# Two-dimensional FFT mixing and a gated FFN on one core: where the column transforms wait, when the last third of the down weights is loaded, and in which blocks the column sums run

## The chip, the core and the metric

The kernel runs on one core of one Trainium2 chip. A core has a matrix engine (TensorE, PE in the profile, with its weight loads listed as PEld), a vector engine (VectorE, DVE), an activation engine (ScalarE, ACT), a general engine (GpSimd, POOL) and a sync engine (SyncE, SP), which in this kernel issues nearly all DMAs. Each engine works through its own list of instructions in order, and the lists meet at semaphores. Matrix products land in PSUM; everything else lies in SBUF, 128 partitions wide. The metric is the device time of one launch in microseconds (us).

## What is computed

The input `x` has 2048 tokens of 576 channels, in bf16. The FFN widens to 4608.

```python
def _A_ref(x, w_r, w_i):                    # a learned filter in the frequency domain
    X = rfft2(x.astype(float32), axes=(-2, -1))
    X = X * (w_r + 1j * w_i)
    return irfft2(X, s=(S, D), axes=(-2, -1)).astype(bfloat16)

def _B_ref(x, w_gate, w_up, w_down):        # gated FFN
    return (_gelu(x @ w_gate) * (x @ w_up)) @ w_down

h  = x + _A_ref(_layernorm(x), A_w_r, A_w_i)
h2 = h + _B_ref(_layernorm(h), B_w_gate, B_w_up, B_w_down)
return h2
```

## The kernel before

**Tiling.** Token `p*16 + h` lies on partition `p`, row `h`, so the residual `h_sb` is 128 partitions x 16 rows x 576 channels. The FFT half (until about 79 us in the profile) does the forward transform, the product with the filter and most of the inverse transform as matrix products with tables of sines. Its last step is a pair: `inv_cols(x, g)` makes the inverse column transform for one of two halves `x` and one of eight pairs of rows `g` in PSUM and evicts it, and `add_rows(g)` with `add_h` (L668 to L694) adds the rows `2g` and `2g+1` of the result to `h_sb`. For `g` = 0 and 1 the evicted values are used at once. For `g` = 2 to 7 they are parked in fp32 as `cw[x, g]` (L576 to L584), and the FFN starts while they are parked. For `x` = 0, and for `g` = 2, each has a tile of its own. The five with `x` = 1 and `g` = 3 to 7 lie in one tile, `cwb` (L640), which shares its place with `wd_c`, the last third of the down weights: `wd_c` can be loaded only when `cwb` has been read for the last time.

`fold(g)` (L656) turns the parked values into bf16 sums and differences, the tile `both`, by four vector instructions (L664 and L665, once for each `x`). These are the column sums. `add_both(g)` issues the eight small matrix products `y_ps` (L678) on `both`, and then two vector adds into `h_sb` (L689). `stats2(h)` takes mean and variance of a finished row on VectorE and the reciprocal root on GpSimd; `norm2(h)` (L703) normalises the row into `hrow`; `flip(h)` (L715) transposes it by DMA into `hl`, the FFN's input, on SP. Rows 0 and 1 are flipped before the FFN, rows 2 and 3 are transposed on TensorE by `turn` at the same time.

**The FFN** runs over four chunks of four rows. A chunk has 36 blocks, one per 128 hidden columns. A block is 18 matrix products `gu` (L814), for gate and up, then GELU on ScalarE (L822) into `g_sb`, then the product with the up half on VectorE (L823) into `P_sb`, which has 36 columns of blocks. After the 36 blocks come 288 products `acc` with the down weights (L834), 12 blocks of hidden columns from each of `wd_a`, `wd_b` and `wd_c`, then the residual add (L846) and the store.

**Buffers and queues.** PSUM has four tiles of one kind ("two", L435), which `gu`, `y_ps` and `acc` take in turn, so the order of their allocation decides who waits for whom. Gate and up weights come in groups of three blocks (`load_gu`, L143, two DMAs of 432 KB each) into three buffers in turn: group `n` can be issued when the last product on group `n-3` is done. All these DMAs, the flips and the down weights stand in one list on SP, in program order: what waits at its head holds up the rest.

**The order around the change.** `todo` (L785) is a plan by block number, counted over all chunks. A block's entries are issued right behind its VectorE product. In the first chunk it places:

- `fold(2)` to `fold(7)` in blocks 2, 3, 4, 5, 6 and 7;
- `add_both(2)` to `add_both(7)` in blocks 4, 10, 16, 22, 28 and 34, and `stats2` of their two rows in the blocks after each;
- `norm2` and `flip` of rows 4 to 7 in blocks 14/15, 17/18, 20/21 and 23/24 (those of later rows in later chunks);
- `last_wd` in block 12, which loads `wd_c`.

Of the kernel before, what the change touches and what calls it, by code (L numbers as in the profile page):

```python
# [10 lines left out]
ALU = mybir.AluOpType  # L11
FP32 = mybir.dt.float32
BF16 = mybir.dt.bfloat16
# [7 lines left out]
P = 128  # L21
S = 2048
H = 16
D = 576
DH = D // 2
J = D // 2 + 1
JP = J + 1
JH = JP // 2
F = 4608
NFT = F // P  # L30
# [10 lines left out]
def kernel_body(  # L41
# [12 lines left out]
    V = nc.vector  # L54
# [11 lines left out]
    def two(name):  # L66
        return psum.tile([P, 2, 512], FP32, name=name, tag="two", bufs=3)
# [75 lines left out]
    def load_gu(g):  # L143
        gc = slice(g % (NFT // FQ) * FQ * P, (g % (NFT // FQ) + 1) * FQ * P)
        t = wgpool.tile([P, NR, FQ * P], BF16, name="wgu", tag="wgu")
        for c, w in ((0, B_w_gate), (1, B_w_up)):
            nc.sync.dma_start(t[64 * c : 64 * c + 64, :, :], w[:, gc].rearrange("(r k) c -> k r c", k=64))
        return t
# [12 lines left out]
    NWA = 12  # L161
    wd_a = keep.tile([P, NWA, D], BF16, name="wd_a")
# [400 lines left out]
    def inv_cols(x, g):  # L563

        ps = two("cs_ps")
        for e in range(2):
            for jt in range(NJT):
                T.matmul(  # L568
                    ps[:, e, 0:JP],
                    lhsT=EO[x][:, e, jt, 2 * g : 2 * g + 2].rearrange("p h e k l -> p (h e k l)"),  # L570
                    rhs=DT[:, jt, :, e, :] if jt < 2 else DI[:, :, e, :],
                    start=(jt == 0),
                    stop=(jt == NJT - 1),
                )
        pv = ps[:, :, 0:JP].rearrange("p t (q a) -> p t q a", q=2)
        if g >= 2:  # L576
            if x == 0 or g == 2:
                cw[x, g] = eop.tile([P, 2, JP], FP32, name=f"cw{x}{g}")[:]
            else:
                cw[x, g] = cwb[:, g - 3]  # L580
            A.activation(
                cw[x, g].rearrange("p t (a q) -> p t q a", q=2), pv, ACT.Copy, scale=Y_SCALE
            )
            return  # L584
        ts = [eop.tile([P, JP], BF16, name=f"cs{x}{g}{t}") for t in range(2)]
        for t in range(2):
            dst = ts[t][:].rearrange("p (a q) -> p q a", q=2)
            if x == 1 and t == 1:
                V.tensor_scalar(dst, pv[:, t], Y_SCALE, None, op0=ALU.mult)
            else:  # L590
                A.activation(dst, pv[:, t], ACT.Copy, scale=Y_SCALE)
        cs[x, g] = ts
# [43 lines left out]
    spw.__exit__(None, None, None)  # L636
    spec.__exit__(None, None, None)
    fp = ctx.enter_context(tc.tile_pool(name="ffn", bufs=1))
    P_sb = fp.tile([P, NFT, 4 * P], BF16, name="P_sb")
    cwb = fp.tile([P, 5, 2, JP], FP32, name="cwb", tag="wd2")[:]  # L640
    wd = [wd_a, fp.tile([P, NWA, D], BF16, name="wd_b")]

    def load_wd(i):
        nc.sync.dma_start(wd[i][:], wd_view[:, i * NWA : (i + 1) * NWA, :])

    def last_wd(h):
        wd.append(fp.tile([P, NWA, D], BF16, name="wd_c", tag="wd2"))
        load_wd(2)

    load_wd(1)  # L650

# [129 lines left out]
    turn(3)  # L781
    inv_cols(1, 6)
    inv_cols(1, 7)

    todo = {}  # L785
    for h in range(4, H):
        b = 6 * (h // 2 - 2)
        if h % 2 == 0:
            todo.setdefault(h // 2, []).append((fold, h // 2))
            todo.setdefault(b + 4, []).append((add_both, h // 2))  # L790
        todo.setdefault(b + 5 + h % 2, []).append((stats2, h))
        b = h // 4 * NFT - NFT + 3 * (h % 4) + 2 + 12 * (h < 8)
        todo.setdefault(b, []).append((norm2, h))
        todo.setdefault(b + 1, []).append((flip, h))

    todo.setdefault(12, []).append((last_wd, 0))

    blk = 0
    groups = pre
    NG = NFT // FQ  # L800
    for tcnk in range(4):
        for gi in range(NG):
            fa = gi * FQ
            w = groups.pop(0)
            n = tcnk * NG + gi + 2
            if 3 <= n < 4 * NG:
                groups.append(load_gu(n))
            for i in range(FQ):

                gu = two("gu")  # L810
                for r in range(NR):
                    for c in range(2):
                        rows = slice(64 * c, 64 * c + 64)
                        T.matmul(  # L814
                            gu[:, c, :],
                            lhsT=w[rows, r, i * P : (i + 1) * P],
                            rhs=hl[tcnk % 2][rows, r, :],
                            start=(r == 0),
                            stop=(r == NR - 1),
                        )  # L820
                g_sb = roll.tile([P, 4 * P], FP32, name="g_sb", tag="g_sb", bufs=3)
                A.activation(g_sb[:], gu[:, 0, :], ACT.Gelu_apprx_tanh)  # L822
                V.tensor_tensor(P_sb[:, fa + i, :], g_sb[:], gu[:, 1, :], ALU.mult)  # L823
                for fn, h in todo.pop(blk, ()):
                    fn(h)
                blk += 1
        for st in range(4):
            h = tcnk * 4 + st
            last = h == H - 1
            acc = two("acc")  # L830
            for c in range(2):
                cc = slice(c * DH, (c + 1) * DH)
                for f in range(NFT):
                    T.matmul(  # L834
                        acc[:, c, 0:DH],
                        lhsT=P_sb[:, f, st * P : (st + 1) * P],
                        rhs=wd[f // NWA][:, f % NWA, cc],
                        start=(f == 0),
                        stop=(f == NFT - 1),
                    )  # L840
                if last:
                    V.tensor_tensor(h_sb[:, h, cc], h_sb[:, h, cc], acc[:, c, 0:DH], ALU.add)  # L842
                    nc.sync.dma_start(out_view[:, h, cc], h_sb[:, h, cc])
            if not last:
                hv = h_sb[:, h, :].rearrange("p (b n) -> p b n", b=2)
                V.tensor_tensor(hv, hv, acc[:, :, 0:DH], ALU.add)  # L846
                if tcnk == 3:
                    nc.sync.dma_start(out_view[:, h, :], h_sb[:, h, :])
        if tcnk < 3:
            nc.sync.dma_start(  # L850
                out_view[:, tcnk * 4 : (tcnk + 1) * 4, :],
                h_sb[:, tcnk * 4 : (tcnk + 1) * 4, :],
            )


@with_exitstack
def kernel(
    ctx: ExitStack,
    tc: tile.TileContext,
    A_x: bass.AP,  # L860
    A_w_r: bass.AP,
    A_w_i: bass.AP,
    B_x: bass.AP,
    B_w_gate: bass.AP,
    B_w_up: bass.AP,
    B_w_down: bass.AP,
    out: bass.AP,
):
    kernel_body(tc, A_x, A_w_r, A_w_i, B_x, B_w_gate, B_w_up, B_w_down, out)
# [30 lines left out]
```

## Time and profile before

| What | us |
|---|---|
| Median of 3 runs | 512.87 |
| All runs | 512.09, 512.87, 512.88 |
| The profiled execution, its device time | 512.41 |
| The profiled execution, its span in the trace | 510.4 |
| FFN, first matrix product of each chunk | 78.9, 189.7, 295.1, 400.6 |
| TensorE clock granted, all slices | 9 tenths or more |

The span is the traced part of the profiled execution; 512.41 - 510.4 = 2.0 us lie around it. Engine times in the profile are busy times; in the chain of waits each piece names the engine and line that the end of the program depended on at that moment, followed back from the last instruction. In a timeline, a row is a run of like instructions: its start, its length, the engine, the line, the tiles, the count, and in brackets how long the engine had been idle before it and what ended that.

### The profile page before, as it was taken

What the parts mean: (1) busy time and instruction counts of PE and PEld (TensorE: products, weight loads), DVE (VectorE), ACT (ScalarE), POOL (GpSimd) and SP (SyncE); (2) the same over time, 40 slices, a digit from 0 to 9 for tenths busy, and PEclk for the clock granted to TensorE, in tenths of its full rate; (3) what the DMA queues carried; (4) which work ended last, traced back from release to release, by engine and by line L of the source; (5) the groups of instructions that cost most, each with busy time, mean ns of one, the idle gap of its engine ahead of it and who ended that gap; (6) DMA issues with size and microseconds to landing.
All of it is one profiled execution on the core that took longest, in us unless ns stands there. A gap on an engine that the chain in (4) does not pass through costs nothing.

```text
span 510.4 us, 9927 instructions
## 1 busy us (share of the span) xinstructions
PE 496.5 (97%) x4357; PEld 291.1 (57%) x4357; DVE 214.1 (42%) x414; ACT 154.6 (30%) x266; POOL 33.2 (6%) x88
## 2 busy tenths in 40 slices
PE   6989999999999999999999999999999999999996
PEld 2557775455447774444467744444577544444775
DVE  8979964967653015433311034433201233333000
ACT  7688985222220003232310023232200132332000
POOL 8700020111110000000000000000000000000000
PEclk9999999999999999999999999999999999999999
DMA  8964063779991009998730079977500578870000
GB/s 281 246 135 140 1 169 67 152 194 200 182 203 25 0 1 220 183 204 161 142 71 0 1 173 195 192 153 161 106 1 0 118 162 156 160 149 2 13 12 25
DMA packets 86091, 60.66 MB, mean 119 GB/s; under 512 B 21920, under 2 KB 84768, under 8 KB 86048
## 3 DMA queue, kind: packets, MB, share of 16 engines
q1 hardware_dynamic: 85760, 58.85, 57.8%
q0 software_dynamic: 288, 1.18, 0.8%
q8 instruction: 34, 0.56, 0.5%
q14 instruction: 9, 0.07, 0.1%
HBM read 52.65 MB, written 2.36 MB: 108 GB/s over the span
## 4 chain that ended last, share of the span: by engine, by line
PE 87%; DVE 7%; DMA 4%; ACT 1%; issue 0%; SPq 0%; POOL 0%; POOLq 0%; ACTq 0%; DVEq 0%
PE gu L814 48%; PE acc L834 28%; DMA wgu<-in_B_w_up_dram 4%; PE cs_ps L568 2%; PE f2t L259 2%; PE pq_ps L442 1%; PE eo_ps L542 1%; PE eo_ps L541 1%; DVE both L665 1%; DVE both L664 1%; DVE P_sb L823 1%; PE y_ps L678 1%; PE f2t L247 1%; PE gh_ps L457 1%; PE gh_ps L458 1%; PE f L268 1%
## 5 line engine op out<-in xcount | busy, mean ns | idle before, releaser
L814 PE MATMUL gu<-Bt,wgu 64*128 64x512 bf16 x2592 | 282.4, 376 | 0.6 <-DMA wgu<-in_B_w_up_dram 0.6
L814 PEld LDWEIGHTS <-wgu 64*128 64x128 bf16 x2592 | 128.4, 94 | 151.5 <-DMA wgu<-in_B_w_up_dram 1.6
L822 ACT ACTIVATE g_sb<-gu 128x512 f32<-128x512 f32 x144 | 86.0, 597 | 304.3 <-PE gu L814 302.9
L823 DVE TENSOR_TENSOR P_sb<-g_sb,gu 128x512 bf16<-128x512 f32 x144 | 98.6, 686 | 154.0 <-ACT g_sb L822 154.0
L834 PEld LDWEIGHTS <-P_sb 128*128 128x128 bf16 x1152 | 112.4, 98 | 30.6 <-issue 2.4
L846 DVE TENSOR_TENSOR h_sb<-h_sb,acc 128x576 bf16<-128x576 bf16 x15 | 11.3, 754 | 118.2 <-PE acc L834 118.2
L834 PE MATMUL acc<-wd_a,P_sb 128*128 128x288 bf16 x384 | 52.3, 286 | 0.5 <-DVE h_sb L842 0.5
L834 PE MATMUL acc<-wd_b,P_sb 128*128 128x288 bf16 x384 | 52.3, 286 | 0.0
L834 PE MATMUL acc<-wd_c,P_sb 128*128 128x288 bf16 x384 | 52.3, 286 | 0.0
L247 PE MATMUL f2t<-h_sb,ident 128*128 128x512 bf16 x41 | 12.9, 441 | 4.4 <-DMA h_sb<-in_A_x_dram 4.4
L442 PE MATMUL pq_ps<-DT,Bt 128*128 128x290 bf16 x64 | 12.4, 287 | 0.0
L703 DVE TENSOR_SCALAR hrow<-h_sb,mv,rstd 128x1152 bf16<-128x1152 bf16 x14 | 12.1, 866 | 0.5 <-POOL rstd L737 0.5
L568 PE MATMUL cs_ps<-DT,EO 128*128 128x290 bf16 x64 | 12.2, 286 | 0.0
L136 POOL TENSOR_TENSOR rstd<-rstd,mhalf 128x1 f32<-128x1 f32 (+2 forms) x17 | 11.9, 697 | 1.4
L541 PE MATMUL eo_ps<-TI,Zt 128*128 128x256 bf16 x48 | 11.5, 272 | 0.4 <-DVE Zt L516 0.4
L247 PEld LDWEIGHTS <-ident 128*128 128x128 bf16 x45 | 4.9, 108 | 11.7 <-issue 5.6
L542 PE MATMUL eo_ps<-TI,Zt 128*128 128x256 bf16 x48 | 11.5, 273 | 0.1
L135 POOL TENSOR_SCALAR rstd<-mv 128x1 f32<-128x1 f32 (+2 forms) x17 | 4.2, 244 | 111.4 <-DVE mv L120 111.2
L568 PEld LDWEIGHTS <-EO 128*128 128x128 bf16 x96 | 9.0, 96 | 3.0 <-issue 0.2
L442 PEld LDWEIGHTS <-Bt 128*128 128x128 bf16 x96 | 9.2, 97 | 2.5
L259 PE MATMUL f2t<-F,xn 128*128 128x256 bf16 x64 | 9.7, 274 | 0.9 <-DVE xn L139 0.9
L450 ACT CAST pq<-pq_ps 128x580 bf16<-128x580 f32 x15 | 9.9, 660 | 0.9 <-PE pq_ps L442 0.8
(133 smaller groups left out, 271.8 us busy)
## 6 DMA issues: line engine op xcount, KB each, us to landing
wgu<-in_B_w_gate_dram SPq DMA_DIRECT2D x48, 432.0 KB, 5.4
wgu<-in_B_w_up_dram SPq DMA_DIRECT2D x48, 432.0 KB, 6.8
h_sb<-in_A_x_dram SPq DMA_DIRECT2D x3, 576.0 KB, 6.6
wd_a<-in_B_w_down_dram SPq DMA_DIRECT2D x1, 1728.0 KB, 9.2
wd_b<-in_B_w_down_dram SPq DMA_DIRECT2D x1, 1728.0 KB, 7.5
wd_c<-in_B_w_down_dram SPq DMA_DIRECT2D x1, 1728.0 KB, 13.0
out_dram<-h_sb SPq DMA_DIRECT2D x3, 576.0 KB, 3.3
WR<-in_A_w_r_dram SPq DMA_DIRECT2D x1, 650.2 KB, 9.4
```

What stands on the lines that cost most here:

```text
L136: G.tensor_tensor(dst[:, sl], dst[:, sl], mhalf[:, sl], ALU.pow)
L247: T.matmul(dst, lhsT=ident[:], rhs=h_sb[:, 2, 0:512], start=True, stop=True)
L259: T.matmul(f2t[:, h % 2, t * 2 * P : (t + 1) * 2 * P], lhsT=x[:, d0 : d0 + P], rhs=F16[:, n : n + 2, :], start=(n == 0), stop=(n == 1),)
L442: T.matmul(ps[:, par, 0:JP], lhsT=Bt[:, t, col], rhs=DT[:, t // 2, par] if t < 4 else DF[:, par], start=(t == par), stop=(t == 4),)
L541: T.matmul(ps[:, b], lhsT=zl(*z0), rhs=TI[:, kk_, 1:3, :], start=True, stop=False)
L542: T.matmul(ps[:, b], lhsT=zl(*z1), rhs=TI[:, kk_, 0:2, :], start=False, stop=True)
L568: T.matmul(ps[:, e, 0:JP], lhsT=EO[x][:, e, jt, 2 * g : 2 * g + 2].rearrange("p h e k l -> p (h e k l)"), rhs=DT[:, jt, :, e, :] if jt < 2 ...
L703: V.tensor_scalar(hrow[:], h_sb[:, h, :].rearrange("p (r k) -> p r k", k=64).unsqueeze(2).to_broadcast([P, NR, 2, 64]), mv2[:, h, 0:1], rs ...
L814: T.matmul(gu[:, c, :], lhsT=w[rows, r, i * P : (i + 1) * P], rhs=hl[tcnk % 2][rows, r, :], start=(r == 0), stop=(r == NR - 1),)
L822: A.activation(g_sb[:], gu[:, 0, :], ACT.Gelu_apprx_tanh)
L823: V.tensor_tensor(P_sb[:, fa + i, :], g_sb[:], gu[:, 1, :], ALU.mult)
L834: T.matmul(acc[:, c, 0:DH], lhsT=P_sb[:, f, st * P : (st + 1) * P], rhs=wd[f // NWA][:, f % NWA, cc], start=(f == 0), stop=(f == NFT - 1),)
```

## The change

`P_sb` is divided: the products of blocks 0 to 21 have one tile, those of blocks 22 to 35 another, which takes the place (tag `P1`) of `cwb`. So `cwb` no longer shares with down weights, and has to be read for the last time before block 22 of the first chunk. The down weights get three tiles of their own. The last third is loaded by a line right before the FFN loop, behind the second `inv_cols(1, 7)`; on SP this stands directly behind the flips of rows 0 and 1, and ahead of the weight groups that the loop loads. `last_wd` and its entry in block 12 are gone. The folds move from blocks 2, 3, 4, 5, 6, 7 to blocks 1, 6, 10, 13, 16, 19. The buffers take the same bytes in all. The number of instructions of every kind on every engine is the same.

```diff
-    P_sb = fp.tile([P, NFT, 4 * P], BF16, name="P_sb")
-    cwb = fp.tile([P, 5, 2, JP], FP32, name="cwb", tag="wd2")[:]
-    wd = [wd_a, fp.tile([P, NWA, D], BF16, name="wd_b")]
+    NP0 = 22
+    P_sb = [fp.tile([P, NP0, 4 * P], BF16, name="P_sb")]
+    cwb = fp.tile([P, 5, 2, JP], FP32, name="cwb", tag="P1")[:]
+    wd = [wd_a] + [fp.tile([P, NWA, D], BF16, name=f"wd_{i}") for i in range(2)]
 
     def load_wd(i):
         nc.sync.dma_start(wd[i][:], wd_view[:, i * NWA : (i + 1) * NWA, :])
 
-    def last_wd(h):
-        wd.append(fp.tile([P, NWA, D], BF16, name="wd_c", tag="wd2"))
-        load_wd(2)
+    def p_sb(f):
+        if f >= NP0 and len(P_sb) == 1:
+            P_sb.append(fp.tile([P, NFT - NP0, 4 * P], BF16, name="P_sb", tag="P1"))
+        return P_sb[f // NP0][:, f % NP0, :]
...
     inv_cols(1, 7)
+    load_wd(2)
 
     todo = {}
     for h in range(4, H):
         b = 6 * (h // 2 - 2)
         if h % 2 == 0:
-            todo.setdefault(h // 2, []).append((fold, h // 2))
+            todo.setdefault((1, 6, 10, 13, 16, 19)[h // 2 - 2], []).append((fold, h // 2))
             todo.setdefault(b + 4, []).append((add_both, h // 2))
...
-    todo.setdefault(12, []).append((last_wd, 0))
...
-                V.tensor_tensor(P_sb[:, fa + i, :], g_sb[:], gu[:, 1, :], ALU.mult)
+                V.tensor_tensor(p_sb(fa + i), g_sb[:], gu[:, 1, :], ALU.mult)
...
-                        lhsT=P_sb[:, f, st * P : (st + 1) * P],
+                        lhsT=p_sb(f)[:, st * P : (st + 1) * P],
```

## The prediction

> **What bounds the kernel now.** First the head of the page, for the engine that fills the span.
>
> ```profile
> PE 496.5 (97%) x4357; PEld 291.1 (57%) x4357; DVE 214.1 (42%) x414; ACT 154.6 (30%) x266; POOL 33.2 (6%) x88
> ```
>
> TensorE is busy for 97%. A change that leaves its instructions as they are can win only where it stands still or works slower than elsewhere. Second, the chain of waits in order of time (start, length, what), from the FFN's start through the second chunk.
>
> ```profile
> 78.95 5.95 PE gu L814 x54
> ...
> 86.24 0.37 DVE both L664
> ...
> 101.25 0.61 DVE P_sb L823
> 101.90 0.65 PE y_ps L678 x7
> ...
> 124.89 10.26 DMA wgu<-in_B_w_up_dram
> ...
> 137.90 9.90 DMA wgu<-in_B_w_up_dram
> 147.85 3.96 PE gu L814 x35
> ...
> 154.34 35.39 PE acc L834 x288
> 189.72 70.04 PE gu L814 x648
> ```
>
> The second chunk is TensorE alone: 648 products in 70.04 us. The first chunk is not: from 84.9 to 101.9 the end hangs on VectorE, which is stuck in folds, and twice later on a weight DMA of some 10 us. Third, the TensorE timeline where the VectorE stretch ends, for what it costs.
>
> ```profile
> 89.09 11.82 PE L814 MATMUL gu<-Bt,wgu 64*128 64x512 bf16 x108
> 100.75 0.28 PE L678 MATMUL y_ps<-both,G 64*128 64x288 bf16 x1
> 101.90 0.65 PE L678 MATMUL y_ps<-both,G 64*128 64x288 bf16 x7 [0.87 <-DVE P_sb L823]
> 102.50 11.83 PE L814 MATMUL gu<-Bt,wgu 64*128 64x512 bf16 x108
> ```
>
> The small products of block 10 need a PSUM tile that the late VectorE product of block 8 still holds. Fourth, SP's timeline, for why the weights come late.
>
> ```profile
> 73.57 2.74 SPq L715 DMA_TRANSPOSE Bt<-hrow  x2
> 84.92 0.63 SPq L147 DMA_DIRECT2D wgu<-in_B_w_gate_dram  x1
> ...
> 106.02 0.57 SPq L644 DMA_DIRECT2D wd_c<-in_B_w_down_dram  x1
> 111.12 0.74 SPq L147 DMA_DIRECT2D wgu<-in_B_w_up_dram  x1
> 112.61 6.71 SPq L715 DMA_TRANSPOSE Bt<-hrow  x1
> 119.43 0.59 SPq L147 DMA_DIRECT2D wgu<-in_B_w_gate_dram  x1
> ```
>
> `wd_c` (1728 KB) goes out at 106.0 and lands 13.0 us later, where `wd_b`, as large, took 7.5. The group issued behind it lands in 11.1 us instead of 6.3 to 6.5 (the four groups before it), the next flip holds SP for 6.71 us, and the group at 119.43 is issued 2.8 us after its buffer came free (block 17 ended at 114.64 + 1.94 = 116.6). This lateness runs on to the groups issued at 124.2 and 137.3, which TensorE waits for.
>
> **What there is to win.** First chunk, 78.95 to 154.34: 75.39 us. Its own work is 70.04 (second chunk) and six sets of eight small products at 0.49 each (126.29 to 126.78), 2.94. The excess is 75.39 - 70.04 - 2.94 = 2.41. Its places in the TensorE timeline: the set of block 10 lasts from 100.75 to 102.50, 1.75, of which 1.26 is too much; 108 products from 126.78 to 138.87 take 12.09 against 11.66 (89.09 to 100.75), 0.43; 107 from 139.58 to 151.53 take 11.95 against 107 x 0.108 = 11.55, 0.40. Together 2.09; 0.32 more lie in the hand-overs around the last two sets and at the chunk's end.
>
> **The folds.** A fold is four instructions of 0.37, 1.47 us. Before, blocks 2 to 7 carry six folds, one `add_both` (1.33) and two `stats2` (0.95 each) besides their six products (0.60 back to back): 8.82 + 1.33 + 1.90 + 3.60 = 15.65 us, in six blocks of 1.94 with one small set, 12.1: VectorE falls 3.5 behind. Now I follow VectorE through the new plan with the same rows (ScalarE's 0.60 and then 0.69 for a product that is not late). Nowhere are two folds adjacent; the densest stretch is blocks 16 to 20, counted from the end of block 16's products: product done 1.3, two adds 2.6, `fold(6)` 4.1, product of 17 4.7, `norm2` and `stats2` 6.5, product of 18 7.1, `stats2` 8.05, product of 19 8.65, `fold(7)` 10.1, product of 20 10.7, `norm2` 11.6, product of 21 12.2. The lag is at most 1.4 us. What TensorE needs: with four PSUM tiles, block 23, which comes after the set of block 22, takes the tile of block 21, at 12.13 + 0.49 = 12.6. So 0.4 us remain there, and more at every other block. The same bookkeeping on the old plan gives a wait of 1.1 at block 10 (1.26 measured), so I trust it to some tenths. The gain of this part is 1.26; bounds 0.6 (a wait of 0.6 comes up around block 22 if each VectorE piece of the stretch is a tenth longer) and 1.26. Folds stay ahead of their small products by three blocks or more, so these never wait for `both`. The flips behind `norm2(5)` to `norm2(7)` are issued up to 1.5 us later than now; in SP's list a weight group stands behind each, due 5.8 us after the one before, and the flip's 2 to 3 us of issue (197.82 and after) still end within 0.3 us of that.
>
> **The last third of the down weights.** The 1728 KB leave the stretch 106 to 119. What is left then, weight groups with a flip between, is what the second chunk has from 191 to 220: there groups land in 7.0 to 8.3 us and TensorE never waits; a group has 11.7 us (two groups of 5.83) from the time its buffer is free. Gain 0.43 + 0.40 = 0.83; bounds 0 and 1.15 (with the 0.32). The load goes to 76.3, when the second flip has been issued (73.57 + 2.74). Its memory is free by then: `wd_b`, beside it in the same pool, went out at 65.74, after the last reader of the FFT's tables. With 7.5 us it lands at 83.8, before the next group is issued at 84.92; the DMA engines are nearly idle between 79 and 84.9. First use is after 155. Behind it on SP stands only that group, which waits for TensorE until 84.92 in any case, so its own 0.4 to 0.6 us of issue are covered. Without this cover the group, which lands by 92.1 (85.59 + 6.5) and is needed at block 9, 89.09 + 4 x 1.94 = 96.9, would still have 4 us to spare.
>
> Its risk is ahead of it: the flip issued last lands 3.3 us after its issue at 74.98, at 78.3, and TensorE's first product needs it at 78.9: 0.6 spare. Down weights issued at 76.3 send bytes from about 77.4 (`wd_b` did 1.1 after issue), while the flip is still on its way. No row shows a flip with a large load behind it. The nearest: weight groups with only a flip behind (issued 195.7 and 301.1) land in 7.0 and 7.3, others, without one (230 to 254), in 6.2 to 6.7: 0.3 to 1.1 later. So the flip lands at 78.6 to 79.4, a cost of 0 to 0.5. I take 0, since the transfer behind is at work only for the flip's last 0.9 us. The Trainium skill, "DMA: Bandwidth & Descriptors", section "Queues, rings and completion order", has each DMA engine consume descriptors of one issuing queue in ring order. By that rule the flip would not be delayed at all, where the rows of later groups say up to 1.1; by the rule the cost is 0, by the rows up to 0.5.
>
> **The divided `P_sb`.** Block 22's product now waits for the last reader of `cwb`, `fold(7)`, three blocks earlier on the same engine: 0. The other products, and `acc`, touch the same bytes in the same order: 0.
>
> **Sum.** 1.26 + 0.83 = 2.09 less. Against the profiled execution 512.41 - 2.1 = 510.3; the median of the runs stands 0.46 higher, 510.8. I forecast 510.5. Bounds of the parts: gain at least 0.6 + 0 - 0.5 = 0.1, at most 1.26 + 1.15 = 2.4.
>
> **The rivals.**
>
> - **The late weights stay.** The flips of blocks 15 to 24 remain in the list and the DMA engines are full with flips and groups also in the second chunk (share 1.18 there). Then only 1.26 is won, or less: 511.4 (from the mean of the two bases, 512.64). Against it: the second chunk has the same mixture and no wait. 0.12.
> - **VectorE still holds PSUM.** The wait of block 10 comes back near block 22, where 0.4 us are spare. With a tenth on all pieces 0.6 come back: 511.2. With more, up to the 1.26 of now, 511.8. 0.09.
> - **Nothing is won.** Both of these, or a late flip of 0.5 with one of them: 512.5. 0.08.
> - **Slower: the flip waits for the down weights.** The flip shares the DMA engines evenly with the 1728 KB and lands as flips beside loads do, in 7.8 us (median): at 74.98 + 7.8 = 82.8, 3.9 after the FFN's start, so 512.64 - 2.1 + 3.9 = 514.4. It decides from a landing of 78.9 + 2.1 = 81.0 on, 6.0 us after issue. For it: every flip beside loads took 6.8 to 10.7. Against it: those were issued behind loads already in flight, this one is ahead. 0.06.
>
> **How the numbers follow.** The forecast has 0.65. The range 509.6 (the lowest of the runs before, 512.09, less 2.4, about) to 512.3 leaves out the slower case, most of "nothing won" and a tail below. A measurement of this kernel can tell about 0.2% (1.03 us) from no change. Faster by more than that: the forecast's 0.65 less a few points, and most of the first two rivals: 0.78. Within: 0.15. Slower: 0.07.
>
> **What would show it.** In the new profile the chain from 79 to the end is TensorE alone, but for the last adds; the six sets of small products take 0.5 each; `acc` starts near 152.3 instead of 154.3; the group behind block 12 lands in 6 to 8 us; no flip of the first chunk holds SP for more than 3.5 us; the second third and the last third of down weights have both landed by 84. I am wrong on the weights if a group is waited for after 130, on VectorE if `y_ps` or `gu` waits for L824, on the flip if the first `gu` starts after 79.0 with a DMA as its releaser.

## The result and the profile after

The changed kernel takes 509.67 us (median of 4 runs, 509.64 to 509.67) against 512.87. The ratio is 0.9941, with a 95% interval from 0.9924 to 0.9958: 0.6% faster. The profiled execution of the changed kernel took 509.67 with a span of 507.4.

The chain of waits of the changed kernel, in order of time (start, length, what), from the FFN's start to the second chunk:

```profile
78.81 9.82 PE gu L815 x90
88.63 0.49 PE y_ps L680 x8
89.12 11.65 PE gu L815 x108
100.77 0.49 PE y_ps L680 x8
101.26 11.65 PE gu L815 x108
112.92 0.49 PE y_ps L680 x8
113.41 11.65 PE gu L815 x108
125.06 0.49 PE y_ps L680 x8
125.55 11.65 PE gu L815 x108
137.21 0.49 PE y_ps L680 x8
137.70 11.65 PE gu L815 x108
149.35 0.49 PE y_ps L680 x8
149.84 1.94 PE gu L815 x18
151.79 35.39 PE acc L835 x288
187.17 70.04 PE gu L815 x648
```

VectorE and the DMA are gone from it. The first chunk lasts 151.79 - 78.81 = 72.98 us, and that is exactly its own work, 70.04 + 6 x 0.49. It was 75.39: all 2.41 us of the excess are won, and nothing anywhere in the FFN is lost for it.

SP's timeline of the changed kernel shows where the weights went:

```profile
73.43 2.76 SPq L717 DMA_TRANSPOSE Bt<-hrow  x2
76.25 0.57 SPq L645 DMA_DIRECT2D wd<-in_B_w_down_dram  x1
84.78 0.63 SPq L147 DMA_DIRECT2D wgu<-in_B_w_gate_dram  x1
...
109.07 0.60 SPq L147 DMA_DIRECT2D wgu<-in_B_w_gate_dram  x1
109.71 1.25 SPq L147 DMA_DIRECT2D wgu<-in_B_w_up_dram  x1
111.47 1.28 SPq L717 DMA_TRANSPOSE Bt<-hrow  x1
115.39 0.60 SPq L147 DMA_DIRECT2D wgu<-in_B_w_gate_dram  x1
```

The load of the last third goes out at 76.25 and lands 8.4 us later, at 84.65, just ahead of the next group. The group at 109.71 lands in 6.7 us (11.1 before), and the flip behind it holds SP for 1.28 us (6.71 before).

Between the two profiled executions 512.41 - 509.67 = 2.74 us are gained: 2.41 in the first chunk, 0.14 because the FFN starts earlier (78.81 for 78.95), and 0.19 after the last add, in the last store and outside the span. No run shows what the change has to do with the last two; the start of the FFN differs by more than that from run to run (78.81 to 79.42 in two profiles of the changed kernel). The remaining 0.46 of the 3.20 between the medians is that the profiled execution of the kernel before was that much shorter than its median.

### The profile page after: what moved, and what is told of

Same layout as the page of the kernel before. It is cut to its first block, busy times and chain, and to the rows that moved or that the text cites. A ratio compares the mean times of both kernels' runs of the same rounds, so it can differ in the third digit from the quotient of the medians.

```text
span 507.4 us, 9925 instructions
## 1 busy us (share of the span) xinstructions
PE 496.0 (98%) x4357; PEld 288.9 (57%) x4357; DVE 213.9 (42%) x414; ACT 154.5 (30%) x266; POOL 33.1 (7%) x88
## 3 DMA queue, kind: packets, MB, share of 16 engines
q0 software_dynamic: 288, 1.18, 0.8%
## 4 chain that ended last, share of the span: by engine, by line
PE 94%; DVE 3%; ACT 1%; issue 0%; POOL 0%; POOLq 0%; ACTq 0%; DVEq 0%
PE gu L815 55%; PE acc L835 28%; PE cs_ps L568 2%; PE f2t L259 1%; PE pq_ps L442 1%; PE y_ps L680 1%; PE eo_ps L542 1%; PE eo_ps L541 1%; PE f2t L247 1%; PE gh_ps L457 1%; PE gh_ps L458 1%; PE f L268 1%; DVE st L119 0%; DVE st L118 0%; DVE m L505 0%
## 5 line engine op out<-in xcount | busy, mean ns | idle before, releaser
L815 PEld LDWEIGHTS <-wgu 64*128 64x128 bf16 x2592 | 126.1, 94 | 152.2 <-issue 1.0
L835 PE MATMUL acc<-wd,P_sb 128*128 128x288 bf16 x768 | 99.3, 286 | 0.0
L136 POOL TENSOR_TENSOR rstd<-rstd,mhalf 128x1 f32<-128x1 f32 (+2 forms) x17 | 11.4, 673 | 1.4
L118 DVE BATCH_NORM_STATS2 st<-h_sb 128x6 f32<-128x288 bf16 x22 | 9.8, 445 | 0.0
```

The lines of the kernel that those rows point to most:

```text
L136: G.tensor_tensor(dst[:, sl], dst[:, sl], mhalf[:, sl], ALU.pow)
L815: T.matmul(gu[:, c, :], lhsT=w[rows, r, i * P : (i + 1) * P], rhs=hl[tcnk % 2][rows, r, :], start=(r == 0), stop=(r == NR - 1),)
L835: T.matmul(acc[:, c, 0:DH], lhsT=p_sb(f)[:, st * P : (st + 1) * P], rhs=wd[f // NWA][:, f % NWA, cc], start=(f == 0), stop=(f == NFT - 1),)
```

## The experiments

### One part of the change at a time

**Only the load is moved.** Down weights before the FFN as in the change, folds where they were:

```diff
-            todo.setdefault((1, 6, 10, 13, 16, 19)[h // 2 - 2], []).append((fold, h // 2))
+            todo.setdefault((2, 3, 4, 5, 6, 7)[h // 2 - 2], []).append((fold, h // 2))
```

> The changed kernel with the folds put back in blocks 2 to 7; the last third of the down weights still goes out before the FFN. Theory (two separate losses): the first chunk, 75.39 us before and 72.98 after, is 72.98 + 1.26 = 74.2, with the one wait for PSUM at block 10 (y_ps on the late VectorE product) and no wait for weights; the time is 509.67 + 1.26 = 510.9. Rival (one loss: the folds alone make the weights late, or the late weights alone count): either 72.98 and 509.7, or 75.4 and 512.1 or more.

511.00 us (510.96 to 511.05, five runs); ratio to the kernel before 0.9961 (0.9946 to 0.9976). The timeline of TensorE around block 10:

```profile
89.29 11.82 PE L815 MATMUL gu<-Bt,wgu 64*128 64x512 bf16 x108
100.95 0.28 PE L680 MATMUL y_ps<-both,G 64*128 64x288 bf16 x1
102.10 0.65 PE L680 MATMUL y_ps<-both,G 64*128 64x288 bf16 x7 [0.87 <-DVE P_sb L824]
```

The wait for PSUM is back to the hundredth, and it is the only wait of the chunk. The chunk lasts 153.40 - 79.15 = 74.25, so 1.27 more than with both parts.

**Only the folds are moved.** The changed kernel with its new buffers, and the load again in block 12:

```diff
     inv_cols(1, 7)
-    load_wd(2)
...
+    todo.setdefault(12, []).append((lambda h: load_wd(2), 0))
```

> The changed kernel with the load of the last third put back in block 12, behind which it stood before; the folds stay spread and all buffers are the new ones. Theory: the load collides with the weight groups and flips as before, one flip holds SP for 5 us or more, two weight groups are waited for; the first chunk is 75.39 - 1.26 = 74.1, so 0.83 to 1.15 longer than the 72.98 after, and the time is 510.5 to 510.8. Rival (the wait of block 10 is what put groups, flips and load in each other's way): no wait for weights, 72.98 and 509.7.

511.24 us (510.95 to 511.39, six runs); ratio 0.9964 (0.9951 to 0.9978). In SP's timeline the flip is stuck again behind load and group:

```profile
104.86 0.63 SPq L645 DMA_DIRECT2D wd<-in_B_w_down_dram  x1
109.37 0.59 SPq L147 DMA_DIRECT2D wgu<-in_B_w_gate_dram  x1
110.01 0.92 SPq L147 DMA_DIRECT2D wgu<-in_B_w_up_dram  x1
111.76 7.05 SPq L717 DMA_TRANSPOSE Bt<-hrow  x1
118.92 0.59 SPq L147 DMA_DIRECT2D wgu<-in_B_w_gate_dram  x1
```

Two groups are waited for, as before. The chunk lasts 153.48 - 79.11 = 74.37, 1.39 more than with both parts. So there are two separate losses: 1.27 and 1.39 when each is put back alone, 2.41 when both are there. They overlap by 0.25. The likely reason is that TensorE reaches a late group sooner if nothing has held it up before: here it waits 0.51 and 0.33 us for the two groups, in the kernel before 0.26 and 0.34. The time is 0.4 above the upper end of what was expected, in part because the FFN starts 0.3 later in this execution than in that of the changed kernel.

**Folds moved, buffers left alone.** The kernel before; `wd_c` must wait for the last fold, in block 19:

```diff
-            todo.setdefault(h // 2, []).append((fold, h // 2))
+            todo.setdefault((1, 6, 10, 13, 16, 19)[h // 2 - 2], []).append((fold, h // 2))
...
-    todo.setdefault(12, []).append((last_wd, 0))
+    todo.setdefault(20, []).append((last_wd, 0))
```

> The kernel before, with its buffers, and only the folds spread as in the change; since the down weights share their place with cwb, their load moves behind the last fold, to block 20. Theory: block 10 no longer waits (1.26 won), but the 1728 KB now stand between the flips of rows 5 and 6, with a weight group behind them: groups come later than before, waits for weights of 1 to 3 us in the first chunk; chunk 74.1 to 77, time 510.8 to 513.8. Rival (the place of the load does not matter once VectorE is on time): 72.98 and about 509.7.

513.67 us (512.29 to 514.05, 12 runs); ratio 1.0007 (0.9996 to 1.0019), the time of before. The timeline of TensorE, profiled in an execution of 512.32:

```profile
125.69 7.93 PE L814 MATMUL gu<-Bt,wgu 64*128 64x512 bf16 x72
133.86 0.39 PE L814 MATMUL gu<-Bt,wgu 64*128 64x512 bf16 x1 [0.24 <-DMA wgu<-in_B_w_gate_dram]
135.66 4.05 PE L814 MATMUL gu<-Bt,wgu 64*128 64x512 bf16 x35 [1.41 <-DMA wgu<-in_B_w_up_dram]
```

The load stands at 123.3, right ahead of a group and a flip. What block 10 no longer loses, block 27 loses: the chunk is 154.69 - 79.11 = 75.58. Four of the twelve executions took 512.29 to 512.46, with a mean granted clock of 0.999 or more, and the trace is of one of them; the other eight, with 0.996 or 0.997, took 513.53 to 514.05, and what cost them the further 1.4 us is in no trace. So with the old buffers this plan gains nothing: the load has to follow the last fold, and there it stands among the flips. Whether it would do no harm later, behind the last flip in block 24, was not tried.

### Where the load hurts

**Ahead of the flips.** The changed kernel with the load one step earlier, directly behind that of the second third:

```diff
     load_wd(1)
+    load_wd(2)
...
     inv_cols(1, 7)
-    load_wd(2)
```

> The changed kernel with the last third issued directly behind the second third at about 66 us, so ahead of the flips of rows 0 and 1 on SP. Theory (a transfer delays what is issued behind it, and hardly what is ahead): 3456 KB at the 350 to 390 GB/s of these loads last until about 77; the flips, issued at 73.4 and 74.8, land at 80 to 83 instead of 78.1, and the FFN starts 1.5 to 4 us late with a DMA as its releaser; time 511 to 513.7. Rival (flips share the engines with a load ahead of them evenly and are done in time): start unchanged at 78.8, time 509.7.

514.87 us (513.04 to 516.49, 12 runs); ratio 1.0041 (1.0025 to 1.0058): slower than the kernel before. The timeline of TensorE, and then its granted clock in stretches of the same execution (stretch, length, busy time and count of PE, PEld, DVE, ACT and POOL, mean granted clock, DMA share, GB/s):

```profile
82.30 11.29 PE L815 MATMUL gu<-Bt,wgu 64*128 64x512 bf16 x90 [3.50 <-DMA Bt<-hrow]
```

```profile
80.00:81.00 1.00, 0.00 (x0) 0.00 (x0) 0.00 (x0) 0.81 (x1) 0.00 (x0) 1.00 0.98 222
81.00:82.30 1.30, 0.01 (x1) 0.04 (x2) 0.00 (x0) 0.00 (x0) 0.00 (x0) 0.79 0.00 0
82.30:83.50 1.20, 1.20 (x6) 0.46 (x8) 0.00 (x0) 0.00 (x0) 0.00 (x0) 0.50 0.00 0
83.50:84.50 1.00, 1.00 (x8) 0.46 (x6) 0.00 (x0) 0.00 (x0) 0.00 (x0) 0.50 0.00 0
84.50:85.50 1.00, 1.00 (x10) 0.41 (x8) 0.00 (x0) 0.00 (x0) 0.00 (x0) 0.67 0.06 16
85.50:86.50 1.00, 1.00 (x12) 0.46 (x10) 0.02 (x1) 0.60 (x1) 0.00 (x0) 1.00 0.00 0
```

The second flip lands at 82.2 instead of 78.1, and TensorE waits 3.50 us. It then pays again: the granted clock is 0.50 up to 84.5 and full only after 85, and the 90 products until the first small set start 11.11 us before it (82.30 to 93.41) where 9.72 is usual (78.88 to 88.60 before). Together 3.50 + 1.39 = 4.9, nearly all of the 4.96 by which this execution, of 514.63, is above the changed kernel's. The median lies above the 513.7 that was expected as the most, since the expectation had no price for the clock; the two executions whose mean granted clock is 1.000, 513.04 and 513.50, lie inside, 3.4 and 3.8 above the changed kernel. The rest of the chunk is free of waits. So the same load, issued 10 us earlier and in front of two small transposes instead of behind them, turns a gain of 0.6% into a loss of 0.4%.

**In block 3.** Ahead of the flips of the first chunk, among weight groups alone:

```diff
-    load_wd(2)
...
+    todo.setdefault(3, []).append((lambda h: load_wd(2), 0))
```

> The changed kernel with the load of the last third in block 3, ten blocks before the first flip of the first chunk. Theory (the load hurts by being in one list with flips, where lateness is handed on from flip to group): one or two groups behind it land in some 10 to 11 us and just make their 11.7, the backlog is gone before the first flip, no wait for weights: first chunk 72.98, time 509.7. Rival (the bandwidth of the stretch is short wherever the 1728 KB stand): waits of 0.8 to 1.2 as with block 12, 510.5 to 511.2.

510.02 us (median of five, 509.97 to 511.34); ratio 0.9960 (0.9946 to 0.9974). From the chain of waits, the chunk's first and last pieces:

```profile
79.10 9.82 PE gu L816 x90
...
152.07 35.39 PE acc L836 x288
```

152.07 - 79.10 = 72.97, no wait at all. The group behind the load lands in 11.1 us and the next one in 9.4, both just in time, and at the first flip the backlog is gone (that flip holds SP for 1.28 us). The 0.30 that the profiled execution (509.97) is above the changed kernel's lies ahead of the FFN, which starts at 79.10 here. So 1728 KB among weight groups cost nothing; among groups and flips they do.

**In block 12, from a list of its own.** As in the run with only the folds moved, but ScalarE issues the load:

```diff
-    def load_wd(i):
-        nc.sync.dma_start(wd[i][:], wd_view[:, i * NWA : (i + 1) * NWA, :])
+    def load_wd(i, q=nc.sync):
+        q.dma_start(wd[i][:], wd_view[:, i * NWA : (i + 1) * NWA, :])
...
-    load_wd(2)
...
+    todo.setdefault(12, []).append((lambda h: load_wd(2, nc.scalar), 0))
```

> The changed kernel with the load of the last third in block 12 again, but issued by ScalarE instead of SyncE, so that groups and flips do not stand behind it in SP's list. Theory (it is the order in SP's list that hands lateness on): flips hold SP for less than 4 us, groups go out on time, no wait or less than 0.3 in all; first chunk 73.0 to 73.3, time 509.7 to 510.0. Rival (the same 16 DMA engines serve both lists, and it is their time that is short): groups still land in 10 us or more and are waited for, 74.1 to 74.4, time 510.8 to 511.2.

511.65 us (511.09 to 513.34, 11 runs); ratio 0.9985 (0.9974 to 0.9995). That is 0.45 above even the rival's range, and my theory falls here. From SP's timeline:

```profile
109.41 0.60 SPq L147 DMA_DIRECT2D wgu<-in_B_w_gate_dram  x1
110.05 0.66 SPq L147 DMA_DIRECT2D wgu<-in_B_w_up_dram  x1
111.80 5.91 SPq L717 DMA_TRANSPOSE Bt<-hrow  x1
117.82 1.15 SPq L147 DMA_DIRECT2D wgu<-in_B_w_gate_dram  x1
```

The load is no longer in this list, and yet the flip holds it for 5.91 us, the group ahead of the flip lands in 11.4 us (11.4 also with the load in SP's list), and the group behind it goes out at 117.82, 2.3 us after block 17 ended (113.59 + 1.94 = 115.53). The chunk lasts 153.52 - 79.15 = 74.37, the same to the hundredth, though TensorE waits in other places (0.60 and 0.24 us for 0.51 and 0.33). So the load need not stand in SP's list to do its harm. What the two lists share are the DMA engines, and I take it that their time is what is short; this is argued, and not shown by a run. The DMA share of the stretch from 112 to 122 us is 1.18 in this run, 1.17 with the load in SP's list and 1.07 in the changed kernel, but the share alone does not decide: the second chunk of the kernel before has 1.18 from 200 to 212 and no wait.

### How far the folds can be pushed together

The changed kernel with the last three folds in blocks 17, 18 and 19:

```diff
-            todo.setdefault((1, 6, 10, 13, 16, 19)[h // 2 - 2], []).append((fold, h // 2))
+            todo.setdefault((1, 6, 10, 17, 18, 19)[h // 2 - 2], []).append((fold, h // 2))
```

> The changed kernel with the last three folds in blocks 17, 18 and 19 instead of 13, 16 and 19. Theory (VectorE falls behind only where its work in a few blocks exceeds their time, and PSUM passes that on): the bookkeeping used in the prediction gives waits of 0.67 before the small products of block 22 and 0.92 before block 23, so a first chunk of 72.98 + 1.6 = 74.6 and a time of 509.67 + 1.6 = 511.3, all of it at blocks 22 and 23. Rival (the plan has far more room than the bookkeeping says, as the waits of the changed kernel are nil): 72.98 and 509.7.

511.61 us (median of 11, 511.26 to 512.84); ratio 0.9977 (0.9968 to 0.9986). The timeline of TensorE at block 22:

```profile
113.25 11.82 PE L815 MATMUL gu<-Bt,wgu 64*128 64x512 bf16 x108
124.90 0.28 PE L680 MATMUL y_ps<-both,G 64*128 64x288 bf16 x1
125.61 0.65 PE L680 MATMUL y_ps<-both,G 64*128 64x288 bf16 x7 [0.43 <-DVE P_sb L824]
126.99 11.83 PE L815 MATMUL gu<-Bt,wgu 64*128 64x512 bf16 x108 [0.73 <-DVE P_sb L824]
```

Both waits stand where they were expected, before the small products of block 22 and before block 23. From 124.90 to 126.99 it takes 2.09 us for what takes 0.49: 1.60 too much, against 0.67 + 0.92 = 1.59 expected. The chunk is 153.40 - 78.81 = 74.59. The hand count of VectorE's pieces against the turn of four PSUM tiles gave this wait to a hundredth; for block 10 of the kernel before it had given 1.1 for 1.26.

### A version that beats both

TensorE's one remaining wait in the FFN is in the last row: its second half of `acc` waits until VectorE has read the first half out of the same PSUM tile. A tile of its own for the second half:

```diff
             acc = two("acc")
             for c in range(2):
+                if last and c:
+                    acc = two("acc")
```

> The changed kernel, and for the last row the second half of acc gets a PSUM tile of its own. In the trace of the changed kernel TensorE idles 0.55 us before that half, until VectorE has read the first half out of the same tile. Theory: the second half starts without a wait, the first half's add and store run beside it, and the time falls by 0.5 us to 509.2. Rival (the last store sets the end and is not earlier by that): 509.6 to 509.7.

509.30 us (median of five, 508.96 to 510.49); ratio to the kernel before 0.9936 (0.9923 to 0.9950). Then beside the changed kernel, on one chip and in the same rounds:

> The changed kernel once more, on the same chip and in the same rounds as the next one, for the direct comparison and for the spread of its times. Theory (the spread of the kernel before, 511.2 to 514.5 over 44 runs, comes mostly from weight groups that are just too late, by a length that depends on the DMA engines): the changed kernel, which waits for no weights, stays within 0.8 us, 509.6 to 510.4, while the kernel before spreads over 2 us or more. Rival (the spread is the chip's): both spread alike.

> The changed kernel with a PSUM tile of its own for the second half of the last row, beside the changed kernel on one chip. From its first trace (FFN start to the last add 425.1 us against 425.8) it is 0.5 to 0.7 us faster than the changed kernel; without an effect on the end the two agree within 0.2.

The changed kernel took 509.70 us (509.65 to 510.28, six runs; ratio 0.9941, 0.9926 to 0.9957), the one with the added tile 509.31 (508.97 to 509.33, six runs; ratio 0.9932, 0.9916 to 0.9947), the kernel before 512.48 (511.82 to 514.51). The last `acc` pieces of TensorE, in the changed kernel and then with the added tile:

```profile
500.18 1.63 PE L835 MATMUL acc<-wd_a,P_sb 128*128 128x288 bf16 x12 [0.55 <-DVE h_sb L843]
501.65 3.10 PE L835 MATMUL acc<-wd,P_sb 128*128 128x288 bf16 x24
```

```profile
498.87 1.63 PE L837 MATMUL acc<-wd_a,P_sb 128*128 128x288 bf16 x12
500.34 3.10 PE L837 MATMUL acc<-wd,P_sb 128*128 128x288 bf16 x24
```

The idle time before the second half is gone. From the FFN's start to the end of the last add it is 425.13 us (78.81 to 503.94) against 425.82 (79.42 to 505.24), 0.69 less. The medians differ by 0.39, 509.31 for 509.70, less than the 0.5 to 0.7 that was expected. The rest lies ahead of the FFN, which does not start at the same time in every execution: where it starts at 78.81 in both, the times are 509.67 (the first profile of the changed kernel) and 508.97 (this one). In these rounds the longest time with the added tile, 509.33, is still below the shortest without, 509.65. The two intervals of the ratios overlap, so the size of this step rests on the traces.

The spread: within 0.63 us the changed kernel agrees with what was expected, and the kernel before spreads over 2.7 in the same rounds. That late weights are the cause was argued, not shown, and two things speak against it. The run with only the folds moved waits for weights too, and spreads over no more than 0.44. And the upper end goes with TensorE's clock: of the 55 executions of the kernel before in the three sets of runs, the nine from 513.45 up have a mean granted clock of 0.996 or less, all others 0.998 or more. The load in block 3 (511.26 and 511.34, both 0.996) and the added tile (510.49, 0.996) have such executions as well, and in their profiles TensorE waits for no weights. What lowers the clock there no trace shows.

## Why the prediction was right

**The folds.** 1.26 was forecast; 1.27 comes back when they alone are put back. (Moved without the load, they bring 75.39 - 74.37 = 1.02, because of the overlap.) The new plan was forecast to leave TensorE free with 0.4 us to spare at block 23, and no engine is waited for in the changed kernel's first chunk. The same bookkeeping placed and sized the waits of a denser plan, 1.59 for 1.60.

**The last third of the down weights.** This is the term that was mis-sized. 0.83 was forecast with 1.15 as its upper bound, because I did not count the 0.32 us in the hand-overs around the last two sets and at the chunk's end. They belong to it: the chunk with only the early load has no excess but the PSUM wait, with every set of small products at 0.49 after it, and the first chunk of the changed kernel is its own work to the hundredth. So the upper bound was the value (75.39 - 74.25 = 1.14 with the load alone). The reading behind the term has to be narrowed. I traced the lateness to a flip that holds SP behind the load. The hold and the late group behind it are there, but with the load in another list both stay: the load's place in SP's list is not what makes them. One sign did not come: the load lands at 84.65, not by 84, since it takes 8.4 us where 7.5 was assumed. Nothing waits for it.

**The flip ahead of the load.** Its cost was forecast at 0, with up to 0.5 by the rows. It lands 3.3 us after its issue, as without the load, and the FFN starts at 78.81, with no DMA as its releaser. Here the trace agrees with the Trainium skill, "DMA: Bandwidth & Descriptors", section "Queues, rings and completion order" (descriptors of one queue are consumed in ring order), and not with the 0.3 to 1.1 from the weight groups with a flip behind them.

**The sum.** 2.09 was forecast for the first chunk, 2.41 were measured. The time of 509.67 lies 0.83 below the point of 510.5 and only 0.07 above the lower end of the range. The parts of the 0.83, counted from the profiled execution: 0.32 are the mis-sized term, 0.18 the choice of a base between that execution and the median (512.41 - 2.09 = 510.32), 0.14 the earlier start of the FFN and 0.19 what lies behind the last add. The last two were in no term, and the whole gain of 2.74 is above the 2.4 that the prediction gave as the most. That the range still held owes something to its lower end, which was counted from the fastest run of the kernel before. The profiled execution was the better base: from the median of 512.87 the same parts give 510.1.

**The rivals.** That late weights stay, and that VectorE holds PSUM near block 22, both have mechanisms that are real: each was brought about by one edit, at 1.39 and 1.60. The slower rival did not come about: behind the flips, the load does not touch them. Its landing time, 82.8, is close to the 82.2 that was measured with the load ahead of the flips, but that is another order, so the likeness says nothing for this rival. Its price for such a landing was too low, since it left out the clock after the wait.

## What to carry to other kernels

When a large load has to go somewhere, look for the stretch in which the DMA engines have nothing to do, and put it behind the small transfers that a busy engine is about to need, not ahead of them; another issuing engine did not make room here. Two buffers that share a place tie two schedules together: moving one user to a place that is needed later freed both here, while moving only the work moved the wait. For work that is spread between blocks, add up the engine's pieces block by block against the turn of the PSUM tiles: here that found the block that would wait, before anything ran.

## What the runs showed of the hardware

TensorE stood idle for 3.50 us, up to 82.30, and its granted clock was 0.50 when it went on. If the clock steps between 1.00 and 0.50, the means of 0.79 (81.00 to 82.30) and 0.67 (84.50 to 85.50) put the fall at 81.75 and the rise at 85.16, so at half clock for 3.4 us. 90 products took 11.11 us for 9.72: a wait of 3.5 us cost 4.9. This agrees with the Trainium skill, "TensorE: Matmul & The Clock Gate", Part 1, by which the clock halves after an idle window of about 3.4 us and is full again after a busy one. But the fall came 3.0 us after the last product had ended (78.51 + 0.28), so less than 3.4 us of idling was enough here. In the profiled executions of the other runs, waits of 0.9 to 1.4 us left the granted clock at 1.00.

A transpose by DMA held the issuing list for 1.3 to 1.8 us in the first chunk of the changed kernel, between weight groups, and for 5.7 to 7.1 us when it was issued while a load of 1728 KB and a weight group were on their way, whichever list the load came from.
